# Four blocks of 240 rows instead of 256 in a mixture of experts behind an attention, and two more products at the start

## The chip, the cores and the metric

The kernel runs on one core of a Trainium2 chip. The metric is the device time of one execution in microseconds (us); lower is better. The time of a version is the median of several runs.

## The reference: what is computed

Two stages. A causal attention over 8 batches, 8 heads, 576 positions and 64 features per head, in which every key gets a bias from a running sum of `max(s, 0)`, gives 8 x 576 = 4608 tokens of 512 features. Each token then goes to exactly one of 8 experts, and the expert's two matrices (512 x 1024 and 1024 x 512) are applied with a ReLU between them:

```python
logits = np.einsum('bsd,de->bse', x, w_gate)
...
            fresh_e = int(np.argmax(logits[b, s]))
            if s == 0 or local_gate[b, s] < 0.5:
                e = fresh_e
            else:
                e = prev_e if prev_e >= 0 else fresh_e
...
            h = np.maximum(x[b, s] @ w1[e], 0.0)
            out[b, s] = p[e] * (h @ w2[e])
```

All numbers are float32. Which expert a token takes is known only on the chip, after its attention row is there. For the inputs of the reference (a fixed seed) the eight experts get 573, 516, 565, 575, 717, 459, 513 and 690 tokens; these counts are worked out from the reference itself.

## The kernel before, in words

**Attention.** `attention` (L736) goes through 32 pairs of heads. `scores` (L863) multiplies keys and queries into PSUM (L874), ScalarE takes the exponent (L875), GpSimd cuts the upper triangle (L860), and `values` (L894) multiplies the weights with V (L904). At the very start, before the first queries and keys have landed, `warm_up(6)` (L806 and L811) issues six products of a zero tile with itself on TensorE; each float32 product is two instructions in the trace, so they stand there as 12 (L809). The first pair's scores come next on TensorE's queue, then six transposes of the key weights (`key_weights`, L824; they wait for `key_exps`, L820, on ScalarE), whose copies on VectorE (L834) release the first weighted V tiles.

**Routing.** While the attention runs, a `Router` counts the tokens of each expert and stores each token's row into a table in DRAM, ordered by expert, with room for every expert.

**Experts.** `Experts` works through a fixed list of 23 units, the string `ORDER`. The sizes of a unit are fixed when the program is built; which expert and which rows of the table a unit takes is data, computed on VectorE and read into registers of the SyncE queue (`piece`, L482), where it becomes the address of a transfer.

- D is a double: 256 rows of one expert. S is 128 rows. M is two halves of 64 rows, T is a half and two quarters of 32 rows, and each piece has its own load of an expert.
- Before: 14 D, 5 S, 1 M, 3 T, in the order `DDDDDDDTDDTDDTDDSSMDSSS`. Units are numbered from 0.
- Every piece loads its expert's two matrices, 2 MB each (`load`, L501, issued at L520 on SyncE's queue), into one of four places; a load is issued when the place's last user is done (`ready` and `loads`, L667 and L679).
- `fetch` (L523) brings the rows from the table, and `turn_x` (L546) transposes them on VectorE (L552).
- `layer1` of D and S (L582) is, for each of 8 chunks of 128 hidden features, 4 products over the 512 features: the expert's first matrix is the stationary side, the rows are the moving side, 256 or 128 columns wide. ScalarE applies the ReLU (L584). As each float32 product is two instructions, a unit has 64 of them.
- `layer2` (L606): for each 128 rows, 8 products (16 instructions) in which the rows' hidden features are stationary (128 columns) and the second matrix moves, 512 columns wide. VectorE scales by the gate (L609) and GpSimd stores the rows to their tokens (L611).
- M and T do both layers with the rows stationary (L573 for the first), in column groups of 64 or 32, and `turn_h` (L586) transposes between them on VectorE.

**Who gets what.** `assign` (L379) takes, per expert, the number of pieces wanted and the number of pieces that there are, and gives the expert and the first row of each piece. It is called for doubles early (2, then 3 of them, while counts are still growing: `assign_early`), for the other 9 doubles (`assign_doubles`, L424), and for singles, halves and quarters (`assign_rest`, L434). What is over after a size goes to the next smaller one. The last two calls are put by hand into layer 1 of unit 1, behind its chunks 2 and 5 (`todo` in `run`, L619). If rows are left over at the end, `over` becomes positive, and a general version of the whole kernel runs behind a branch.

**Order of the work.** Every engine works through its own queue in program order. Behind the assignment on VectorE's queue stand `turn_x(2)`, which unit 2 needs, and the scaling of unit 1's results.

Of the kernel before, what the change touches and what calls it, by code (L numbers as in the profile page):

```python
# [10 lines left out]
I32 = mybir.dt.int32  # L11
Act = mybir.ActivationFunctionType
Alu = mybir.AluOpType
# [4 lines left out]
P = 128  # L18
B, H, S, DH = 8, 8, 576, 64
D = H * DH  # L20
E, F = 8, 1024
N = B * S
# [31 lines left out]
ROWS = E * CAP + 2 * P  # L54
EMPTY = 1 << 20
DOUBLE, SINGLE, HALF, QUARTER = 2 * P, P, P // 2, P // 4
EARLY = (2, 3)
PIECES = {"D": (DOUBLE,), "S": (SINGLE,), "M": (HALF, HALF), "T": (HALF, QUARTER, QUARTER)}
ORDER = "DDDDDDDTDDTDDTDDSSMDSSS"
UNITS_OF = {size: sum(PIECES[u].count(size) for u in ORDER) for size in (DOUBLE, SINGLE, HALF, QUARTER)}  # L60
PLACES = 4
SUM_MIN, SUM_MAX, ONE_MAX, END_MAX = 1e-19, 1e25, 1e12, 1e29

# [51 lines left out]
class Router:  # L115
# [294 lines left out]
    def assign_early(self, i):  # L410
# [3 lines left out]
        if i == 0:  # L414
            self.start, self.early = self.t("start", [P, E]), []
            of, self.used, _ = self.assign("a0", n, None, EARLY[0], DOUBLE)
        else:
# [4 lines left out]
        self.early.append(of)  # L422

    def assign_doubles(self):  # L424
        v = self.nc.vector
        self.counted()
        n = self.shifted("n1", 8)
        v.tensor_tensor(n, n, self.used, op=Alu.subtract)
        v.tensor_scalar(self.start, self.used, float(DOUBLE), None, Alu.mult)
        self.doubles, used, _ = self.assign("b", n, self.start, UNITS_OF[DOUBLE] - sum(EARLY), DOUBLE)  # L430
        v.tensor_tensor(self.used, self.used, used, op=Alu.add)
        v.tensor_scalar(self.start, self.used, float(DOUBLE), None, Alu.mult)

    def assign_rest(self):  # L434
        v = self.nc.vector
        n = self.shifted("n2", 7, QUARTER - 1)
        v.scalar_tensor_tensor(n, self.used, -2.0, n, Alu.mult, Alu.add)
        self.singles, used, _ = self.assign("c", n, self.start, UNITS_OF[SINGLE], SINGLE)
        v.scalar_tensor_tensor(self.used, self.used, 2.0, used, Alu.mult, Alu.add)
        v.tensor_scalar(self.start, self.used, float(SINGLE), None, Alu.mult)  # L440
        n = self.shifted("n3", 6, QUARTER - 1)
        v.scalar_tensor_tensor(n, self.used, -2.0, n, Alu.mult, Alu.add)
        self.parts, used, _ = self.assign("d", n, self.start, UNITS_OF[HALF], HALF)
        v.scalar_tensor_tensor(self.used, self.used, 2.0, used, Alu.mult, Alu.add)
        v.tensor_scalar(self.start, self.used, float(HALF), None, Alu.mult)
        n = self.shifted("n4", 5, QUARTER - 1)
        v.scalar_tensor_tensor(n, self.used, -2.0, n, Alu.mult, Alu.add)
        self.quarters, _, end = self.assign("q", n, self.start, UNITS_OF[QUARTER], QUARTER)
        self.over = self.t("over", [P, 1])
        v.tensor_scalar(self.over, end[:, E - 1 :], -float(UNITS_OF[QUARTER]), 0.0, Alu.add, Alu.max)  # L450


class Experts:
    def __init__(self, ctx, tc, w1, w2, out, table, router):
# [16 lines left out]
        loads = 0  # L471
        for kind in ORDER:
            at = []
            for size in PIECES[kind]:
                at.append((size, count[size]))
# [6 lines left out]
    def piece(self, u, i, row):  # L482
        size, n = self.units[u][1][i]
        r = self.router
        if size == DOUBLE:
            if n < sum(EARLY):
                j = int(n >= EARLY[0])
                of, n = r.early[j], n - j * EARLY[0]
            else:
                of, n = r.doubles, n - sum(EARLY)  # L490
        else:
            of = getattr(r, {SINGLE: "singles", HALF: "parts", QUARTER: "quarters"}[size])
        return self.nc.values_load(of[0:1, row, n : n + 1], engines=[ET.SP], min_val=0,
                                   max_val=E * CAP if row else E - 1,
                                   skip_runtime_bounds_check_because="clamped when it was counted")
# [27 lines left out]
    def fetch(self, u):  # L523
        if u >= len(self.units):
            return
        nc = self.nc
        kind = self.units[u][0]
        n = 2 if kind == "D" else 1
        xq = self.xq[u] = self.xqs.tile([P, 2 * DOUBLE // DH, XW], F32, name="xq")
        gi = self.gi[u] = self.sm.tile([P, 2, 2], F32, name="gi")  # L530

        def get(to, of):
            self.tc.add_to_no_dep_group("gets", nc.sync.dma_start(to, of).ins)

        first = 0
        for i, size in enumerate(PIECES[kind]):
            r = self.piece(u, i, 1)
            src = self.table[bass.ds(r, size)]
            t = slice(first // 32, (first + size) // 32)
            for a in range(4):  # L540
                get(xq[32 * a : 32 * a + 32, t, :], src[:, a, :].rearrange("(t i) f -> i t f", i=32))
            p = min(size, P)
            get(gi[first : first + p, :n, :], src[:, 0, XW - 2 :].rearrange("(n p) f -> p n f", p=p))
            first += size

    def turn_x(self, u):  # L546
        if u >= len(self.units):
            return
        n = 8 if self.units[u][0] == "D" else 4
        xq = self.xq.pop(u)  # L550
        xT = self.xT[u] = self.xts.tile([P, DK, DOUBLE], F32, name="xT")
        self.nc.vector.transpose(xT[:, :, : 32 * n].rearrange("p c (t i) -> p t c i", i=32),  # L552
                                 xq[:, :n, : P].rearrange("p t (c i) -> p t c i", i=32))
# [8 lines left out]
    def layer1(self, u, c):  # L562
        nc, mm = self.nc, self.nc.tensor.matmul
        kind, _, ls = self.units[u]
        xT = self.xT[u]
        if kind in "MT":
            if c == 0:
                self.hs[u] = self.fp.tile([P, F], F32, name="hs")
            if c < 2:
                ps = self.ps_m.tile([P, 512], F32, name="hp", tag="m")  # L570
                for k in range(DK):
                    for d, l in self.groups(u):
                        mm(ps[d, :], lhsT=xT[:, k, d], rhs=self.ws[l][0][:, k, c * 512 : c * 512 + 512],  # L573
                           start=(k == 0), stop=(k == DK - 1))
                nc.scalar.activation(self.hs[u][:, c * 512 : c * 512 + 512], ps, Act.Relu)  # L575
            return
        w = DOUBLE if kind == "D" else SINGLE
        if c == 0:
            self.hT[u] = self.fp.tile([P, FK, DOUBLE], F32, name="hT")
        ps = self.ps_h.tile([P, DOUBLE], F32, name="hp")  # L580
        for k in range(DK):
            mm(ps[:, :w], lhsT=self.ws[ls[0]][0][:, k, c * P : c * P + P], rhs=xT[:, k, :w],  # L582
               start=(k == 0), stop=(k == DK - 1))
        nc.scalar.activation(self.hT[u][:, c, :w], ps[:, :w], Act.Relu)  # L584
# [12 lines left out]
    def layer2(self, u, between=None):  # L597
        nc, mm = self.nc, self.nc.tensor.matmul
        kind, _, ls = self.units[u]
        hT = self.hT.pop(u)  # L600
        gi = self.gi.pop(u)
        for n in range(2 if kind == "D" else 1):
            ps = self.ps_y.tile([P, D], F32, name="yp")
            for k in range(FK):
                for d, l in self.groups(u):
                    mm(ps[d, :], lhsT=hT[:, k, n * P + d.start : n * P + d.stop], rhs=self.ws[l][1][:, k, :],  # L606
                       start=(k == 0), stop=(k == FK - 1))
            y = self.yp.tile([P, D], F32, name="y")
            nc.vector.tensor_scalar_mul(y, ps, gi[:, n, 1:2])  # L609
            nc.gpsimd.memset(self.router.gap, 0.0)  # L610
            put = nc.gpsimd.indirect_dma_start(  # L611
                out=self.out[:, :], out_offset=bass.IndirectOffsetOnAxis(ap=gi.bitcast(I32)[:, n, 0:1], axis=0),
                in_=y[:, :], element_offset=0, bounds_check=N - 1, oob_is_err=False, in_offset=None).ins
            self.tc.declare_no_dep(put, group="outs", reason="no two rows of the output are the same")
            self.tc.add_to_no_dep_group("outs", put)
            if between and not n:
                between()
# [118 lines left out]
def attention(ctx, tc, q, k, v, s, wx, ident, recs, wend, router, experts):  # L736
    nc = tc.nc
# [68 lines left out]
    def warm_up(n):  # L806
        warm = banks("warm")[:, 0]
        for i in range(n):
            mm(warm[:, :P], lhsT=zero, rhs=zero, start=True, stop=True)  # L809

    warm_up(6)  # L811

    nc.vector.tensor_scalar(s_sb, s_sb, 0.0, None, Alu.max)
    nc.vector.tensor_tensor_scan(cum, ones, s_sb, 0.0, op0=Alu.mult, op1=Alu.add)
# [122 lines left out]
    for g in range(NG - 1):  # L937
        m = HP * GB // 2 * (g + 1)
# [17 lines left out]
    m = NPAIR // 2  # L956
# [621 lines left out]
```

## Time and profile before

| what | value |
|---|---|
| median of 3 runs | 733.62 us (733.31 to 734.97) |
| the profiled execution | 753.2 us |
| its span, first to last instruction | 751.5 us |
| TensorE busy | 733.7 us, 98% of the span |
| VectorE, ScalarE, GpSimd busy | 253.2, 166.4, 207.0 us |
| layer 1 with rows moving (L582) | 1216 instructions, 234.1 us |
| layer 2 (L606) | 752 instructions, 259.3 us |
| mean traffic with HBM | 248 GB/s |
| granted TensorE clock, mean | 0.995 |

In the trace PE is TensorE's matmul, PEld its loading of the stationary side, DVE is VectorE, ACT ScalarE, POOL GpSimd and SP SyncE; a q behind the name means the engine's queue (it waits or issues a transfer). An instruction is named by the line of the kernel, what it writes and what it reads. The chain of waits is the work that ended last, followed back from the end: each piece is either the instruction before it on its engine, or what released it. What is not in the chain costs no time as long as it stays out of it. Layer 1 of the first unit begins at 223.6 us of the span; the experts fill the rest.

### The profile page before, as it was taken

Reading aid. Unit: us, or ns where it says so; the run is one execution under the profiler, and the core shown is the slowest. Engines: PE = TensorE matmul, PEld = TensorE weight load, DVE = VectorE, ACT = ScalarE, POOL = GpSimd, SP = SyncE. Lnnn points to the kernel's source line nnn. Section 1 sums busy time; section 2 is a strip of 40 time slices with the busy share of each in tenths; the row PEclk is TensorE's granted clock in tenths of the full one; section 3 lists DMA queues with packets and bytes.
Section 4 is the critical chain, followed back from the end, with each engine's and each line's share of the span. In section 5 each row is a group of like instructions: output and inputs, shape, how many; then the busy total and the mean of one; then the engine's idle time right before and its main releaser. Section 6 shows DMA issues by size and latency. Waiting matters only on the chain.

```text
span 751.5 us, 16161 instructions
## 1 busy us (share of the span) xinstructions
PE 733.7 (98%) x6517; PEld 502.5 (67%) x6517; DVE 253.2 (34%) x684; ACT 166.4 (22%) x355; POOL 207.0 (28%) x453
## 2 busy tenths in 40 slices
PE   9999999999989999999999999999999999999996
PEld 6888877878877567567657375537645676637674
DVE  4656668677756462101100511040132001050110
ACT  4545555355331011011001010101110111101110
POOL 3443367577575254340100001010101001000110
PEclk9999999999999999999999999999999999999998
DMA  8454464665639997698546979996999955899100
GB/s 280 165 176 159 142 199 150 199 214 170 187 88 363 356 397 221 235 425 211 229 145 204 375 235 423 303 388 255 427 309 381 426 193 228 283 386 359 36 15 32
DMA packets 57204, 187.28 MB, mean 249 GB/s; under 512 B 11869, under 2 KB 32093, under 8 KB 49568
## 3 DMA queue, kind: packets, MB, share of 16 engines
q1 hardware_dynamic: 50224, 165.91, 62.6%
q0 software_dynamic: 6800, 20.09, 7.0%
q8 instruction: 53, 0.87, 0.5%
q14 instruction: 31, 0.25, 0.1%
q10 hardware_dynamic: 96, 0.15, 0.1%
HBM read 165.50 MB, written 20.88 MB: 248 GB/s over the span
## 4 chain that ended last, share of the span: by engine, by line
PE 96%; issue 1%; DVE 1%; POOL 1%; DMA 1%; ACT 0%; SPq 0%; POOLq 0%; ACTq 0%
PE yp L606 34%; PE hp L582 31%; PE po L904 13%; PE ps L874 12%; PE hp L573 4%; PE lp L216 2%; DMA qb<-in_q_dram 1%; POOL table L348 0%; ACT e L875 0%; PE pos L300 0%; POOL e L860 0%; PE pos L301 0%; DVE xb L912 0%; SPq L769 0%; DVE y L609 0%
## 5 line engine op out<-in xcount | busy, mean ns | idle before, releaser
L606 PE MATMUL yp<-w2b,hT 128*128 128x512 f32 (+2 forms) x752 | 259.3, 593 | 0.0
L582 PE MATMUL hp<-xT,w1b 128*128 128x256 f32 (+1 forms) x1216 | 234.1, 353 | 0.0
L582 PEld LDWEIGHTS hp<-xT,w1b 128*128 128x128 f32 x1216 | 206.8, 191 | 32.9 <-issue 7.8
L606 PEld LDWEIGHTS yp<-w2b,hT 128*128 128x128 f32 (+2 forms) x752 | 107.9, 167 | 141.0 <-issue 139.6
L611 POOL DMA_INDIRECT out_dram<-y,gi x37 | 36.5, 986 | 416.8 <-DVE y L609 397.8
L584 ACT ACTIVATE hT<-hp 128x256 f32<-128x256 f32 (+1 forms) x152 | 54.0, 355 | 434.0 <-PE hp L582 420.8
L609 DVE TENSOR_SCALAR y<-yp,gi 128x512 f32<-128x512 f32 x37 | 27.6, 747 | 307.6 <-PE yp L606 307.6
L904 PE MATMUL po<-vg,e 128*64 128x66 f32 x3200 | 104.9, 223 | 7.0 <-issue 5.6
L875 ACT ACTIVATE e<-ps 128x768 f32<-128x768 f32 (+1 forms) x128 | 97.1, 837 | 47.1 <-PE ps L874 46.4
L904 PEld LDWEIGHTS po<-vg,e 128*64 128x64 f32 x3200 | 98.7, 138 | 13.0 <-issue 10.9
L874 PE MATMUL ps<-qb,kb 64*128 64x192 f32 (+4 forms) x768 | 98.1, 406 | 0.9 <-DMA qb<-in_q_dram 0.5
L874 PEld LDWEIGHTS ps<-qb,kb 64*128 64x128 f32 x768 | 66.2, 190 | 31.8 <-ACT e L875 15.2
L860 POOL TENSOR_SCALAR_AFFINE_SELECT e<-e 128x256 f32<-128x256 f32 (+1 forms) x160 | 67.3, 445 | 51.9 <-ACT e L875 50.8
L348 POOL DMA_INDIRECT table<-xb,idx x54 | 54.5, 1010 | 19.5 <-issue 17.2
L593 DVE STREAM_TRANSPOSE hT<-hs 32x256 f32<-32x256 f32 x64 | 27.9, 436 | 74.8 <-ACT hs L575 74.0
L854 DVE TENSOR_TENSOR vg<-va,wk 128x256 f32<-128x256 f32 x64 | 41.4, 711 | 0.0
L911 DVE RECIPROCAL recs<-po 128x12 f32<-128x12 f32 x64 | 13.5, 211 | 64.4 <-PE po L904 47.9
L552 DVE STREAM_TRANSPOSE xT<-xq 128x1024 f32<-128x1024 f32 (+1 forms) x23 | 23.7, 1028 | 16.5 <-DMA xq<-table 15.9
L573 PE MATMUL hp<-w1b,xT 128*32 128x512 f32 (+1 forms) x224 | 28.3, 594 | 0.0
L912 DVE TENSOR_TENSOR xb<-po,recs 128x384 f32<-128x384 f32 (+1 forms) x48 | 22.0, 458 | 1.9 <-POOL e L860 0.3
L573 PEld LDWEIGHTS hp<-w1b,xT 128*32 128x32 f32 (+1 forms) x224 | 8.1, 114 | 17.7 <-issue 17.6
L923 DVE STREAM_TRANSPOSE xt<-xb 128x576 f32<-128x576 f32 x24 | 17.1, 751 | 0.0
(229 smaller groups left out, 195.5 us busy)
## 6 DMA issues: line engine op xcount, KB each, us to landing
w2b<-in_w_dram SPq DMA_DIRECT2D x30, 2048.0 KB
w1b<-in_w_dram SPq DMA_DIRECT2D x29, 2048.0 KB
va<-in_v_dram SPq DMA_DIRECT2D x32, 320.0 KB
kb<-in_k_dram SPq DMA_DIRECT2D x31, 288.0 KB
qb<-in_q_dram SPq DMA_DIRECT2D x31, 288.0 KB
xq<-table SPq DMA_DIRECT2D x56, 130.0 KB
w1b<-in_w_dram SPq DMA_DIRECT2D x4, 512.0 KB
xq<-table SPq DMA_DIRECT2D x20, 65.0 KB
```

Of the source, the lines that this page charges most:

```text
L348: put = self.nc.gpsimd.indirect_dma_start(out=self.halves, in_=src, element_offset=0, in_offset=None, out_offset=bass.IndirectOffsetOnAxis ...
L573: mm(ps[d, :], lhsT=xT[:, k, d], rhs=self.ws[l][0][:, k, c * 512 : c * 512 + 512], start=(k == 0), stop=(k == DK - 1))
L582: mm(ps[:, :w], lhsT=self.ws[ls[0]][0][:, k, c * P : c * P + P], rhs=xT[:, k, :w], start=(k == 0), stop=(k == DK - 1))
L584: nc.scalar.activation(self.hT[u][:, c, :w], ps[:, :w], Act.Relu)
L593: self.nc.vector.transpose(hT[32 * a : 32 * a + 32, :, 32 * r : 32 * r + 32], hs[32 * r : 32 * r + 32].rearrange("p (c i) -> p c i", i=P)[ ...
L606: mm(ps[d, :], lhsT=hT[:, k, n * P + d.start : n * P + d.stop], rhs=self.ws[l][1][:, k, :], start=(k == 0), stop=(k == FK - 1))
L611: put = nc.gpsimd.indirect_dma_start(out=self.out[:, :], out_offset=bass.IndirectOffsetOnAxis(ap=gi.bitcast(I32)[:, n, 0:1], axis=0), in_= ...
L854: nc.vector.tensor_tensor(vg[:, to].rearrange("p c h e -> p (c h) e")[:, :, :DH], va[:, :c].rearrange("p c h e -> p (c h) e"), wk[:, n, to ...
L860: nc.gpsimd.affine_select(out=ap, in_=ap, compare_op=Alu.is_ge, fill=0.0, base=base, pattern=n, channel_multiplier=-1)
L874: mm(ps[:, h, at : at + z - a], lhsT=kb[d, key : key + P], rhs=qb[d, a:z], start=True, stop=True)
L875: nc.scalar.activation(e, ps, Act.Exp, scale=scale)
L904: mm(po[d, j - j0, :], lhsT=weights_of(n, c, j, h), rhs=vgs[n % NV][:, c if j < 2 * G1 else G1 + c, h, :], start=(c == 0), stop=(c == last))
```

## The change

Four of the 14 doubles become units of a new kind N, of 240 rows (`NARROW`): units 6, 9, 12 and 15. An N unit is a double in everything but this: the moving side of layer 1 is 240 columns wide, and the second part of layer 2 has 112 rows, so 112 stationary columns, and the scaling and the store take 112 rows. It still fetches, turns and indexes 256 rows.

Which experts get an N is decided on the chip in `assign_doubles`: `few` is 1 for an expert whose count minus one has bit 4 clear, which means that its last 32 rows hold 16 rows or fewer. Such an expert gets one N, if it still wants a double and there is one left. From then on, its count is raised by 16 (`cnt`), and the first row of its later pieces is lowered by 16 (`less`, `behind`). The remaining doubles, singles, halves and quarters are assigned as before.

The `warm_up` at the start issues 8 products instead of 6.

```diff
+NARROW = DOUBLE - QUARTER // 2
-ORDER = "DDDDDDDTDDTDDTDDSSMDSSS"
+ORDER = "DDDDDDNTDNTDNTDNSSMDSSS"
...
     def assign_doubles(self):
         v = self.nc.vector
         self.counted()
         n = self.shifted("n1", 8)
         v.tensor_tensor(n, n, self.used, op=Alu.subtract)
+        bit = self.s("bit", [P, E], I32)
+        v.tensor_scalar(bit, self.cnt, -1, None, Alu.add)
+        v.tensor_scalar(bit, bit, 4, None, Alu.logical_shift_right)
+        v.tensor_scalar(bit, bit, 1, None, Alu.bitwise_and)
+        few = self.s("few", [P, E])
+        v.tensor_copy(few, bit)
+        v.tensor_scalar(few, few, -1.0, 1.0, Alu.mult, Alu.add)
+        v.tensor_tensor(few, few, n, op=Alu.min)
         v.tensor_scalar(self.start, self.used, float(DOUBLE), None, Alu.mult)
+        self.narrows, narrow, _ = self.assign("w", few, self.start, UNITS_OF[NARROW], NARROW)
+        v.tensor_tensor(n, n, narrow, op=Alu.subtract)
+        v.scalar_tensor_tensor(self.start, narrow, float(NARROW), self.start, Alu.mult, Alu.add)
         self.doubles, used, _ = self.assign("b", n, self.start, UNITS_OF[DOUBLE] - sum(EARLY), DOUBLE)
         v.tensor_tensor(self.used, self.used, used, op=Alu.add)
-        v.tensor_scalar(self.start, self.used, float(DOUBLE), None, Alu.mult)
+        v.tensor_tensor(self.used, self.used, narrow, op=Alu.add)
+        self.less = self.t("less", [P, E])
+        v.tensor_scalar(self.less, narrow, float(DOUBLE - NARROW), None, Alu.mult)
+        whole = self.s("whole", [P, E])
+        v.tensor_tensor(whole, self.base, self.less, op=Alu.add)
+        v.tensor_tensor(self.cnt, whole, self.base0, op=Alu.subtract)
+        self.behind(DOUBLE)
+
+    def behind(self, size):
+        v = self.nc.vector
+        v.tensor_scalar(self.start, self.used, float(size), None, Alu.mult)
+        v.tensor_tensor(self.start, self.start, self.less, op=Alu.subtract)
...
 -        v.tensor_scalar(self.start, self.used, float(SINGLE), None, Alu.mult)
+        self.behind(SINGLE)
...
-        v.tensor_scalar(self.start, self.used, float(HALF), None, Alu.mult)
+        self.behind(HALF)
...
-            of = getattr(r, {SINGLE: "singles", HALF: "parts", QUARTER: "quarters"}[size])
+            of = getattr(r, {NARROW: "narrows", SINGLE: "singles", HALF: "parts", QUARTER: "quarters"}[size])
...
             r = self.piece(u, i, 1)
+            size = DOUBLE if size == NARROW else size
...
-        w = DOUBLE if kind == "D" else SINGLE
+        w = PIECES[kind][0]
...
-        for n in range(2 if kind == "D" else 1):
+        for n in range(2 if kind in "DN" else 1):
+            m = NARROW - P if kind == "N" and n else P
             ps = self.ps_y.tile([P, D], F32, name="yp")
             for k in range(FK):
                 for d, l in self.groups(u):
+                    d = slice(d.start, min(d.stop, m))
                     mm(ps[d, :], lhsT=hT[:, k, n * P + d.start : n * P + d.stop], rhs=self.ws[l][1][:, k, :],
                        start=(k == 0), stop=(k == FK - 1))
             y = self.yp.tile([P, D], F32, name="y")
-            nc.vector.tensor_scalar_mul(y, ps, gi[:, n, 1:2])
+            nc.vector.tensor_scalar_mul(y[:m], ps[:m], gi[:m, n, 1:2])
...
-    warm_up(6)
+    warm_up(8)
```

## The prediction

> **What bounds the kernel now.** I read first the shares of the chain that ended last, then the same chain in order of time (start, length, what):
>
> ```profile
> PE 96%; issue 1%; DVE 1%; POOL 1%; DMA 1%; ACT 0%; SPq 0%; POOLq 0%; ACTq 0%
> ```
>
> ```profile
> 6.35 4.28 PE ps L874 x20
> ...
> 381.95 13.73 PE yp L606 x32
> 395.68 13.81 PE hp L582 x64
> 409.49 7.00 PE hp L573 x64
> 416.50 20.93 PE yp L606 x96
> ...
> 702.67 7.14 PE hp L582 x64
> ```
>
> From 233.8 us to 744.8 us there is nothing but TensorE in this chain, one unit closing on the next: 395.68 + 13.81 = 409.49. A transfer, VectorE or ScalarE are never what ends last there. So in the experts' stage an instruction taken from TensorE comes off the end, until something else is late. Layer 1 of a double (L582) is 13.81 us for 64 instructions, 215.8 ns each for 256 columns; of a single (the last line) 7.14 / 64 = 111.6 ns for 128; layer 2 is 13.73 / 32 = 429.1 ns for 512. Between 256 and 512 a column costs 213.3 / 256 = 0.833 ns, between 128 and 256 it costs 0.814 ns.
>
> The groups of instructions, kept apart by shape, tell whether stationary loads matter (busy us, mean ns, idle before):
>
> ```profile
> L606 PE MATMUL yp<-w2b,hT 128*128 128x512 f32 x528 | 230.3, 593 | 0.0
> L606 PEld LDWEIGHTS yp<-w2b,hT 128*128 128x128 f32 x528 | 99.6, 190 | 120.6 <-issue 120.0
> ```
>
> A load takes 190 ns and the loader then idles about 240 ns, within the 429 ns of one product: it lies wholly beside the product.
>
> At the start TensorE is slow. Its timeline there:
>
> ```profile
> 2.78 1.27 PE L809 MATMUL warm<-xb 128*128 128x128 f32 x5
> 4.55 1.65 PE L874 MATMUL ps<-qb,kb 64*128 64x384 f32 x4 [0.49 <-DMA qb<-in_q_dram]
> 7.79 0.96 PE L874 MATMUL ps<-qb,kb 64*128 64x448 f32 x2
> 8.54 0.96 PE L874 MATMUL ps<-qb,kb 64*128 64x448 f32 x2
> 9.28 0.74 PE L874 MATMUL ps<-qb,kb 64*128 64x320 f32 x2
> ```
>
> Warming products of 128 columns begin 0.213 us apart (five in 1.27 us, of which the last takes 0.42), against 0.112 us in a single. Pairs of scores of 448 columns begin 0.75 us apart, 1.67 ns a column: half speed. It ends at about 10.2 us.
>
> **What the Trainium skill says.** "TensorE: Matmul & The Clock Gate", section "Back-to-back issue gap": a product's spacing at full clock is its columns at 2.4 GHz plus about 2.5 ns. With two array cycles a column, which is what this trace shows (0.833 ns), 240 columns are 200 + 2.5 = 202.5 ns; 256 would be 215.8, as measured. Section "LDWEIGHTS (loading the stationary operand)": loading time goes with the number of stationary columns, whatever the rows. The trace agrees in direction (190, 138 and 110 ns for 128, 64 and 32 columns), with a fixed part. Section "What's actually happening": the array runs at half clock until one window of about 3.4 us has been busy, and the windows run freely, not from the kernel's start. The trace agrees on the length: the clock falls once later, and from the stretches
>
> ```profile
> 232.00:234.00 2.00, 1.75 (x29) 1.49 (x30) 0.20 (x1) 0.00 (x0) 0.00 (x0) 0.52 0.93 374
> 234.00:236.00 2.00, 2.00 (x7) 1.62 (x7) 1.80 (x11) 0.00 (x0) 0.00 (x0) 0.62 1.06 448
> ```
>
> (the third number from the end is the granted clock) it was at half from 232.08 to 235.52, 3.4 us. Counting 65 such windows of 3.413 us back from 232.1 gives 10.25, just where the first speed-up stands. So windows ended here at 3.42, 6.84 and 10.25 us.
>
> **The change part by part.**
>
> *Do four experts qualify?* From the counts 573, 516, 565, 575, 717, 459, 513, 690, bit 4 of the count minus one is clear for 516, 717, 459 and 513: four experts. After the five early doubles each of them still wants one, so all four N are filled. Six doubles are then wanted and five are there, as ten and nine before. Singles 5, halves 6 wanted of 5, quarters 6 of 6 come out as before, nothing is left over. So the list of units does the same work in the same places, with 16 empty rows less in four of them.
>
> *Layer 1 of four N.* 16 columns less are 13.3 ns (0.833 x 16) an instruction, 64 instructions a unit, 4 units: 3.41 us; with 0.814 ns it is 3.33. That an odd width is charged by the column is seen in the attention: 66 columns, two column groups side by side, take 5.98 us for 200 instructions, 59.8 ns a pair against 55 + 2.5. The stationary loads here (190 ns) are as many as before and singles stream past them at 111.6 ns, so 202.5 ns is not below what they need. I take 3.4, all on the path.
>
> *Layer 2's second half, 112 stationary columns.* Still 16 instructions of 512 moving columns, 429 ns each: no gain. A load between 138 and 190 ns, about 177. No row shows 112 columns, so both ends: 0 if it hides like 128, or 64 loads x 0.177 = 11.3 us if none did. Nothing below zero, as the product's time is set by its moving side. I take 0: 64 and 32 columns hide as well. Scaling (747 ns) and store (986 ns) of 112 rows are off the path: 0.
>
> *Assignment on VectorE.* It adds 27 instructions in `assign_doubles` (6 for `few`, 14 for one more `assign`, 7 around) and 2 in `assign_rest`. The block now:
>
> ```profile
> 258.43 0.16 DVE L365 TENSOR_TENSOR cnt<-base,base 128x8 int32<-128x8 f32 x1
> ...
> 273.86 0.15 DVE L450 TENSOR_SCALAR over<-qend 128x1 f32<-128x1 f32 x1
> 274.31 1.25 DVE L552 STREAM_TRANSPOSE xT<-xq 128x1024 f32<-128x1024 f32 x1 [0.30 <-issue]
> 278.44 0.75 DVE L609 TENSOR_SCALAR y<-yp,gi 128x512 f32<-128x512 f32 x1 [2.89 <-PE yp L606]
> ```
>
> 80 instructions in 15.6 us, 0.195 each; 29 more are 5.7 us (4.9 to 7.0 with 0.17 to 0.24). Queued behind are `turn_x(2)`, then the scaling of unit 1. The turn ends at 281.3 instead of 275.6; unit 2's layer 1 wants it at 285.3, so 4 us of cover stay. The scaling at 278.4 slips to about 281.3; its PSUM buffer, one of two, is next wanted by unit 2's layer 2 at 299.3, and GpSimd's store of it and the table stores behind slip 3 us, for a fetch that SyncE issues at 341.8. SyncE first reads N's numbers for the load at 314.0 and the other doubles' at 299.3; both stand by about 268. Cost 0; if the cover were gone, the excess over 9.7 us would go straight to the path.
>
> *Do the weights keep up?* An N is ahead of each T, the unit with three loads, and takes 0.85 us from their lead. The tightest is unit 13:
>
> ```profile
> 518.32 2.56 SPq L520 DMA_DIRECT2D w2b<-in_w_dram  x3
> 521.46 0.33 SPq L520 DMA_DIRECT2D w1b<-in_w_dram  x1
> ```
>
> Four loads of 2.1 MB, 8.4 MB at the 409 to 422 GB/s that the stretches from 520 to 540 show, are 20 us: landed at about 541, used from 548.4. Seven us of cover against 0.85: cost 0. Fetches are unchanged.
>
> *Two more warming products.* Four instructions x 0.213 = 0.85 us: TensorE's stream of them ends at 4.71 instead of 3.85, and the first scores start at 4.71 instead of 4.55. This 0.16 is hidden, as the scores after the fourth wait for a transfer that lands at 6.30. What it may bring: in the window 3.42 to 6.84 TensorE streamed 0.43 + 1.41 + 0.49 = 2.33 of 3.41 us, 68%, and the clock stayed low. With the gap filled it is 3.07 us, 90%. No row shows whether 90% is enough. If so, full clock from 6.84, and the first pair's scores end up to 3.41 / 2 = 1.7 us earlier. ScalarE's timeline limits what comes through:
>
> ```profile
> 8.04 0.81 ACT L875 ACTIVATE e<-ps 128x768 f32<-128x768 f32 x1 [0.99 <-PE ps L874]
> 12.40 0.32 ACT L851 COPY vg<-wk 128x14 f32<-128x14 f32 x2 [0.91 <-DVE wk L834]
> ```
>
> Only the 0.99 us can shrink ahead of the key exponents; the transposes at 10.46 then come 1.2 earlier at most, and the rest follows. Ends: 0 (not raised) and 2.0 (an execution whose windows lie worse, where the second pair's scores were slow too). I take 1.0.
>
> *Sum.* 3.4 + 1.0 = 4.4 us: the profiled execution goes from 753.2 us to 748.8 (its span from 751.5 to 747.1). The median of the runs is 19.6 us lower than the profiled execution; columns over clock are the same in both, so I take off the same 4.4: 733.6 to 729.2.
>
> **The rivals.**
> - *Width only, the clock is not raised earlier.* For: 90% is not a full window, and windows lie differently in each execution. Against: the filled gap is nearly all that was missing. 733.6 - 3.4 = 730.2.
> - *Width does not pay* (240 columns cost what 256 do). For: no row shows 240. Against: 66 columns cost by the column. 732.6 with the warming, 733.6 without: no change.
> - *Slower: loads of 112 stationary columns are not drawn under the running product.* Place: 16 loads in each N's second half. Price 0.177 us x 64 = 11.3, so 733.6 - 4.4 + 11.3 = 740.5. It decides from 4.4 / 64 = 69 ns shown per load, and makes the kernel slower by over 0.2% from 92 ns. Against: every other width hides.
> - *It doesn't do what it says*: rows left over start the general kernel, and the time at least doubles (over 1467 us). The counts above leave this only if the chip chose otherwise.
>
> **How the numbers follow.** About 0.2%, 1.5 us, is what can be told from no change. Both parts work: 55%, 729.2. Width only: 32%, 730.2. Width does not pay: 7%. Exposed loads: 5%. Rows left over or the assignment's cover gone: 1%. Range: from 1.8 us below the first case (warming worth 2.0, and 0.8 for the scatter, as the runs shown span 1.66 us) to 1.2 above the second (scatter, and 232 us's fall of the clock, at most 1.7 us, which may come or go): 727.4 to 731.4; it leaves out 13% of cases and some tails. Faster 0.87, same 0.07, slower 0.06.
>
> **What would show it.** Layer 1 of units 6, 9, 12, 15 at 12.96 us instead of 13.81; their layer 2 still 13.73; no wait other than TensorE's in the chain from unit 1 on; the turn for unit 2 ending near 281 less the start's gain; pairs of 448 columns under 0.4 us apart at the start. Wrong would be: layer 2 of N above 13.8, a gap before unit 2, a weight wait before a T.

## The result, and the profile after

The changed kernel takes 731.51 us (median of 6 runs, 730.73 to 731.85); the kernel before, run beside it, takes 734.28 us (6 runs). The medians differ by 2.8 us. The ratio is 0.9957 with a 95% interval of 0.994 to 0.9973, which is 3.2 us faster, between 2.0 and 4.4. A second comparison on a chip with about the same times gave 0.9954 (0.9941 to 0.9967), and two on chips on which both kernels take longer gave 0.995 (0.9932 to 0.9968) and 0.9945 (0.9931 to 0.996). The profiled execution of the changed kernel took 731.85 us with a span of 730.1 us.

One thing has to be known before the two profiles are laid side by side. The profile of before (753.2 us) evidently came from another chip than its three runs (733.62 us). On such a chip the same kernel takes 750 us in its other executions as well (experiment `b6_again`). So the 21 us between the two spans are mostly the chip, not the change, and stages are compared by their lengths, not by their place in the span. There is no trace of the kernel before from a chip on which it takes 734 us.

The shares of the chain that ended last are as before:

```profile
PE 96%; DMA 1%; ACT 1%; DVE 1%; issue 1%; POOL 0%; POOLq 0%; DVEq 0%; ACTq 0%
```

The same chain in order of time (start, length, what), at unit 6, which is an N, then the next two pieces, and later unit 15, an N with its own layer 2 behind it:

```profile
377.54 12.96 PE hp L608 x64
390.50 7.00 PE hp L599 x64
397.50 20.93 PE yp L634 x96
...
583.47 12.96 PE hp L608 x64
596.43 13.73 PE yp L634 x32
```

Layer 1 of an N is 12.96 us where a double's was 13.81; its layer 2 is 13.73 as before, and the pieces still close on one another (583.47 + 12.96 = 596.43). The groups by shape (busy us, mean ns, idle before) show the two new shapes:

```profile
L608 PE MATMUL hp<-xT,w1b 128*128 128x240 f32 x256 | 52.5, 366 | 0.0
L634 PE MATMUL yp<-w2b,hT 128*112 128x512 f32 x64 | 28.1, 592 | 0.0
L634 PEld LDWEIGHTS yp<-w2b,hT 128*112 128x112 f32 x64 | 11.3, 177 | 16.1 <-issue 16.1
```

The loads of 112 stationary columns take 177 ns, as estimated, and the loader idles 16.1 us before 64 of them, 0.25 us each: they hide under the product, whose mean is 592 ns as the others' is 593.

VectorE's timeline over the longer assignment, and TensorE's at the place that waits for it:

```profile
240.29 0.16 DVE L366 TENSOR_TENSOR cnt<-base,base 128x8 int32<-128x8 f32 x1
...
261.06 0.15 DVE L475 TENSOR_SCALAR over<-qend 128x1 f32<-128x1 f32 x1
261.15 1.25 DVE L578 STREAM_TRANSPOSE xT<-xq 128x1024 f32<-128x1024 f32 x1
```

```profile
266.96 3.40 PE L608 MATMUL hp<-xT,w1b 128*128 128x256 f32 x15
```

From the first instruction of the assignment to the turn it is 20.9 us instead of 15.9, and the turn ends at 262.4, 4.6 us before unit 2 begins.

TensorE's timeline at the start:

```profile
6.58 0.54 PE L902 MATMUL ps<-qb,kb 64*128 64x448 f32 x2
6.96 0.54 PE L902 MATMUL ps<-qb,kb 64*128 64x448 f32 x2
```

The pairs of 448 columns begin 0.38 us apart instead of 0.75: the clock has risen. The trace's record of the granted clock has it at 5.12 us, against 10.23 in the trace of before.

### The profile page after: what moved, and what is told of

It reads as the page before. It is cut to its first block, busy times and chain, and to the rows that moved or that the text cites. A ratio compares the mean times of both kernels' runs of the same rounds, so it can differ in the third digit from the quotient of the medians.

```text
span 730.1 us, 16198 instructions
## 1 busy us (share of the span) xinstructions
PE 719.0 (98%) x6521; PEld 496.6 (68%) x6521; DVE 258.4 (35%) x713; ACT 165.4 (23%) x355; POOL 206.1 (28%) x453
## 4 chain that ended last, share of the span: by engine, by line
PE 96%; DMA 1%; ACT 1%; DVE 1%; issue 1%; POOL 0%; POOLq 0%; DVEq 0%; ACTq 0%
PE yp L634 35%; PE hp L608 31%; PE po L932 12%; PE ps L902 11%; PE hp L599 4%; PE lp L217 1%; DMA table<-xb,idx 1%; ACT e L903 1%; PE warm L837 1%; DVE xb L940 0%; PE pos L301 0%; POOL e L888 0%; POOL table L349 0%; PE pos L302 0%; DVE y L637 0%
## 5 line engine op out<-in xcount | busy, mean ns | idle before, releaser
L634 PE MATMUL yp<-w2b,hT 128*128 128x512 f32 (+3 forms) x752 | 259.3, 593 | 0.0
L608 PE MATMUL hp<-xT,w1b 128*128 128x256 f32 (+2 forms) x1216 | 229.8, 349 | 0.0
L634 PEld LDWEIGHTS yp<-w2b,hT 128*128 128x128 f32 (+3 forms) x752 | 107.1, 166 | 141.8 <-issue 140.2
L610 ACT ACTIVATE hT<-hp 128x256 f32<-128x256 f32 (+2 forms) x152 | 53.4, 352 | 425.4 <-PE hp L608 425.4
L637 DVE TENSOR_SCALAR y<-yp,gi 128x512 f32<-128x512 f32 (+1 forms) x37 | 27.6, 745 | 304.8 <-PE yp L634 298.5
L932 PE MATMUL po<-vg,e 128*64 128x66 f32 x3200 | 98.5, 223 | 2.2 <-issue 1.2
L932 PEld LDWEIGHTS po<-vg,e 128*64 128x64 f32 x3200 | 95.5, 138 | 5.1 <-issue 3.7
L902 PE MATMUL ps<-qb,kb 64*128 64x192 f32 (+4 forms) x768 | 94.1, 397 | 0.5 <-ACT e L903 0.3
## 6 DMA issues: line engine op xcount, KB each, us to landing
w1b<-in_w_dram SPq DMA_DIRECT2D x29, 2048.0 KB, 10.1
```

The source lines that it names most:

```text
L902: mm(ps[:, h, at : at + z - a], lhsT=kb[d, key : key + P], rhs=qb[d, a:z], start=True, stop=True)
L932: mm(po[d, j - j0, :], lhsT=weights_of(n, c, j, h), rhs=vgs[n % NV][:, c if j < 2 * G1 else G1 + c, h, :], start=(c == 0), stop=(c == last))
```

## The experiments

Theory A: the width is worth all of its 3.4 us, and the two more warming products little. Theory B: the warming is worth 1.0 us or more, and a part of the width is eaten by a wait. The runs stand in three groups, each on one chip, on which the kernel before was timed as well; ratios are against it. In the first two groups it takes about 750 us, in the third (from `w8_move` on) 734.5.

| run | what it is | median us | before | ratio (95%) |
|---|---|---|---|---|
| b6_again | before, once more | 751.53 | 750.05 | 1.0009 (0.9992 to 1.0027) |
| w6_width | N units, 6 products | 747.31 | 750.05 | 0.9959 (0.9945 to 0.9973) |
| b8_warm | doubles, 8 products | 750.67 | 750.05 | 0.9998 (0.9981 to 1.0015) |
| w8_again | the changed kernel | 746.98 | 750.05 | 0.9950 (0.9932 to 0.9968) |
| w8_n224 | layer 1 of N on 224 columns; leaves out its last 16 rows | 743.46 | 750.63 | 0.9918 (0.99 to 0.9936) |
| w6_width2 | as w6_width | 745.11 | 750.63 | 0.9936 (0.9918 to 0.9954) |
| w8_again2 | the changed kernel | 746.07 | 750.63 | 0.9945 (0.9931 to 0.996) |
| w8_late | loads 1 and 2 of the experts put behind chunk 5 | 745.95 | 750.63 | 0.9946 (0.9931 to 0.9962) |
| w8_move | last projection two chunks later | 730.46 | 734.47 | 0.9943 (0.993 to 0.9955) |
| w8_again3 | the changed kernel | 731.11 | 734.47 | 0.9954 (0.9941 to 0.9967) |
| w0_width | N units, no warming product | 731.54 | 734.47 | 0.9960 (0.9945 to 0.9975) |
| w8_spin | 60 more additions on VectorE | 739.66 | 734.47 | 1.0069 (1.0052 to 1.0087) |

### b6_again: which execution was the exception

No edit.

> The kernel before, once more, for its trace and as a measure of the scatter: ratio 1.000 within 0.2%. Theory A (the first traced execution of it, 753 us, was an exception): its span here is about 732 us, layer 1 of the first unit begins near 211 to 213 us instead of 223.6, and no stretch at half clock stands between attention and experts, or one that costs up to 4 us. Theory B (tracing costs 20 us in that version): 751 us again.

Neither theory as it was worded. Its traced execution has a span of 751.5 us, but the others of this kernel take 750 to 751 us here too (medians). Tracing costs nothing that can be seen; the chip does. Between attention and experts its chain has this, as the trace of before had:

```profile
229.55 1.17 issue
230.72 0.25 PE lp L216
...
233.65 9.71 PE hp L582 x40
243.36 6.87 PE yp L606 x16
```

"issue" is TensorE waiting for nothing that the profile shows. In the changed kernel's trace from the other chip the same stretch is without it:

```profile
215.04 1.46 PE lp L217 x64
216.50 8.83 PE hp L608 x40
225.33 6.87 PE yp L634 x16
```

From the beginning of the first unit to that of the second it is 34.1 us in the trace of before and 29.9 us in this one. 0.88 of the difference is 9.71 against 8.83 for the same 40 instructions: in the trace of before the clock stood at half from 232.10 to 235.51 us, over the first 1.75 us of them. This stretch is a part of what the two chips differ by; the larger part, 223.6 against 209.7 us, lies before the first unit.

### w6_width and b8_warm: one part each

```diff
-    warm_up(8)
+    warm_up(6)
```

> The four units of 240 rows alone, with six warming products. Theory A (the width is worth all of its 3.4 us, the two more warming products bring nearly nothing in most executions): 3.4 us less than before, ratio 0.9954. Theory B (the warming brings its 1.0 us and the width is eaten by a wait): 1.5 to 2 us less, ratio about 0.9975. In the trace both want layer 1 of an N at 12.96 us.

0.9959 is 3.1 us, the 3.4 of Theory A within its interval (2.0 to 4.1 us); layer 1 of the N units stands at 12.96 us.

```diff
-    warm_up(6)
+    warm_up(8)
```

> Eight warming products alone, all doubles of 256 rows. Theory A: within 0.5 us of before, ratio 0.9995 to 1.0005, although the clock rises in the first pair's scores in the trace. Theory B: 1.0 us less or more, ratio 0.9986 or below. Scores of 448 columns begin 0.37 us apart if the clock has risen, 0.75 if not.

0.9998: no difference, between 1.4 us faster and 1.1 slower. Its trace has the clock up at 5.66 us, and scores of 448 columns 0.37 us apart. So the clock does what the warming is for, and the time does not show it. That is as Theory A had it, but the interval still holds the 1.0 us of Theory B.

### w8_again, w6_width2, w8_again2: is there anything in the warming?

No edits beyond those above.

> The changed kernel, once more, on the same chip as the three others: ratio 0.9957 as measured (2.8 to 3.4 us less). Theory A: equal to the width alone within 0.5 us. Theory B: 1 us below the width alone.

> The width alone once more, beside the changed kernel on this chip. Theory A (warming is worth the 1.0 us that the trace shows at the start): 1.0 us slower than the changed kernel. Theory B (the start's gain is given back before the experts begin): equal to it within 0.3 us.

> The changed kernel once more: ratio 0.995 to 0.9957. Theory A: 1.0 us below the width alone. Theory B: equal within 0.3 us.

By the medians, the changed kernel is 0.3 us below the width alone in the first group, as Theory A of `w8_again` had it, and 1.0 above it in the second, which no theory had. All 28 executions of the width alone have a mean of 747.0 us, the 33 of the changed kernel 746.6: 0.4 us, with a standard error of 0.45. `b8_warm` has 0.0 with 0.46 in the same way (14 executions against 48). Together that is 0.2 with 0.3: 1.0 us is unlikely, though neither comparison alone rules it out.

In the traces from these chips the lead is there. The second slot of scores (behind the first two pairs' scores) begins at 20.2 to 20.7 us with six products (four traces) and at 19.1 to 19.8 with eight (five traces), and the first unit begins at 222.5 us in the mean of the four against 221.6 in the mean of the five, still 0.9 us apart. Single traces of one version differ by up to 2 us at that point, so the traces do not tell where the lead goes, or whether it goes.

### w8_n224: is every column paid?

```diff
-        w = PIECES[kind][0]
+        w = PIECES[kind][0] - (16 if kind == "N" else 0)
...
+            if kind == "N":
+                nc.gpsimd.memset(self.hT[u][:, :, w:NARROW], 0.0)
```

> The changed kernel with layer 1 of the four N units cut to 224 columns (it leaves out layer 1 of the last 16 rows of each N; those hidden features are set to zero). Theory A (every column is paid at 0.833 ns, nothing else is near): layer 1 of an N at 64 x 189.2 ns = 12.11 us, another 3.4 us less than the changed kernel, ratio about 0.991. Theory B (something else than the columns is close, such as loads or the ReLU): 12.5 us or more, less than 1.7 us gained.

The chain of its trace:

```profile
390.42 12.11 PE hp L610 x64
```

12.11 us, exactly as expected: 13.81, 12.96 and 12.11 for 256, 240 and 224 columns, 0.85 us for each 16. Its median is 2.6 us below the changed kernel's on the same chip, against 3.4 in the trace; the means differ by 3.3 with a standard error of 0.8, which covers it. Down to 224 columns nothing else limits layer 1.

### w8_late: are the weights' transfers to blame for the waits at the hand-over from attention to experts?

```diff
-            (0, 0): [lambda: self.load(0, 1, behind=self.hT[0][0:1, 0, 0:1]), lambda: self.load(1), lambda: router.assign_early(1), lambda: self.load(2)],
+            (0, 0): [lambda: self.load(0, 1, behind=self.hT[0][0:1, 0, 0:1])],
+            (0, 5): [lambda: self.load(1), lambda: router.assign_early(1), lambda: self.load(2)],
```

> The changed kernel, but the weights of experts' loads 1 and 2 (8 MB) are issued after chunk 5 of unit 0's layer 1 instead of after chunk 0. Theory A (at the hand-over from attention to experts TensorE is starved by that burst of transfers, goes idle, and its clock falls to half for 3.4 us in some executions): the waits at L217 between 227 and 232 us and the half-clock stretch vanish, 1 to 3 us less than the changed kernel and less scatter. Theory B (the waits there have another cause): same as the changed kernel within 0.5 us.

Equal to the changed kernel (745.95 against 746.07), and the waits stand where they stood, with the half clock behind them. Its chain:

```profile
228.28 0.37 issue
228.64 0.34 PE lp L217 x3
228.99 0.39 issue
...
232.08 10.52 PE hp L608 x40
```

But the edit did not take the transfers away from this place. SyncE's timeline, and the stretch of 2 us in which the waits begin (the last two numbers are the busy share of the DMA engines and GB/s):

```profile
225.65 0.35 SPq L545 DMA_DIRECT2D w1b<-in_w_dram  x1
226.37 0.54 SPq L545 DMA_DIRECT2D w2b<-in_w_dram  x1
242.78 0.33 SPq L545 DMA_DIRECT2D w1b<-in_w_dram  x1
```

```profile
228.00:230.00 2.00, 0.86 (x20) 0.23 (x8) 0.00 (x0) 0.00 (x0) 1.70 (x3) 1.00 1.02 431
```

Load 1 went out at 225.65 and 226.37 us, as in the trace of `w8_again2` (225.02 and 226.46): SyncE has a queue of its own, and nothing in it waits for chunk 5. Only load 2 came later, at 242.78 instead of 227.93, because it waits for `assign_early`, which was moved with it. So the DMA engines were busy all through the waits, and Theory A was not put to the test. Two other traces speak against it. In the trace of before, TensorE has waits of the same kind between 189.3 and 191.0 us, where the DMA engines are busy for 0.26 of the time:

```profile
189.30:191.00 1.70, 0.86 (x14) 0.55 (x13) 0.00 (x0) 0.00 (x0) 0.97 (x1) 1.00 0.26 95
```

And `w8_move`, below, goes through the same instructions without a wait beside a full stream of transfers, though on the other kind of chip.

### w8_move, w8_again3, w0_width: a chip without those waits

```diff
-            (0, 2): [lambda: router.product(last, self.xts_of, self.banks, (1,)),
+            (0, 4): [lambda: router.product(last, self.xts_of, self.banks, (1,)),
```

> The changed kernel, but the last group's projection and what hangs on it (product, logits, codes and the two turns) stands behind chunk 4 of unit 0's layer 1 instead of chunk 2. Theory A (TensorE's waits of 2 to 3 us at L217 come from its queue of short instructions not being filled fast enough right behind the attention, and lead to the fall of the clock): fewer or no waits at L217, no stretch at half clock, 1 to 3 us less than the changed kernel. Theory B (they come with the product wherever it stands): same as the changed kernel within 0.5 us.

> The changed kernel once more, as the measure for the others on this chip: ratio 0.9945 to 0.9957.

These runs were made on a chip of the shorter time, whose traces have no wait at L217 and no half clock there, before the move or after it. So neither theory was put to the test. The stretch with L217 in the trace of `w8_move` has TensorE busy for all of its 1.40 us, at a DMA share of 1.05:

```profile
217.50:218.90 1.40, 1.40 (x65) 1.25 (x65) 0.00 (x0) 0.38 (x1) 1.24 (x3) 1.00 1.05 431
```

Its 730.46 us is the lowest of all and 0.65 us below the changed kernel, with intervals that overlap. From the first unit on, both traces last 520.2 us, so the move itself gave nothing that the trace shows.

```diff
-    warm_up(8)
```

> The four N units without any warming product. Theory A (six products never raised the clock before the first pair's scores were through, so none is as good as six): clock up at about 10.2 us in the trace as with six, time equal to the width alone, 0 to 1.0 us above the changed kernel. Theory B (warming in itself is worth something beyond that): the clock rises later, past 11 us, and it is 2 us or more above the changed kernel.

731.54 against 731.11 us: 0.4 us, as on the other chips, and no more certain (the means differ by 0.5 with a standard error of 0.6). Theory A's time came, Theory B's 2 us did not; the clock did neither. Without any warming the clock rose at 8.18 us, earlier than in the four traces with six products (10.1 to 10.4), as TensorE's timeline shows:

```profile
4.46 1.65 PE L901 MATMUL ps<-qb,kb 64*128 64x384 f32 x4 [4.46 <-DMA qb<-in_q_dram]
...
7.83 0.72 PE L901 MATMUL ps<-qb,kb 64*128 64x448 f32 x2
8.38 0.54 PE L901 MATMUL ps<-qb,kb 64*128 64x448 f32 x2
```

The second pair of 448 columns begins 0.55 us behind the first, between the 0.75 of half clock and the 0.38 of full clock: the rise at 8.18 us falls into the first.

### w8_spin: what the cover before unit 2 is worth

```diff
-            (1, 5): [router.assign_rest],
+            (1, 5): [router.assign_rest, self.spin],
...
+        for _ in range(60):
+            self.nc.vector.tensor_tensor(pad, pad, self.router.less, op=Alu.add)
```

> The changed kernel with 60 more small additions on VectorE behind the assignment, about 12 us. The cover left before unit 2 is 4.6 us in the changed kernel's trace: layer 1 of unit 2 begins 7 to 8 us later, with a wait of that length for the turn of its rows, and nothing of it is won back. If instead VectorE's block were not on that path: no change.

TensorE's timeline, and after it the stretches of 5 us (granted clock third from the end):

```profile
272.61 2.93 PE L608 MATMUL hp<-xT,w1b 128*128 128x256 f32 x6 [7.19 <-DVE xT L578]
```

```profile
265.00:270.00 5.00, 0.42 (x1) 0.00 (x0) 4.15 (x26) 0.00 (x0) 0.00 (x0) 0.87 0.81 275
270.00:275.00 5.00, 2.39 (x6) 1.95 (x7) 4.71 (x13) 0.00 (x0) 1.40 (x3) 0.50 0.43 180
```

The 60 additions took 12.0 us. From unit 1 to unit 2 it is 34.9 us instead of 27.5: 7.4 us longer, which is 12.0 less the 4.6 of cover. The idle TensorE also lost its clock, from 268.7 to 275.5 us, which cost some 1.5 us more (from unit 2 to unit 6 it is 111.9 us against 110.4). Together that is 8.9; the median of its two runs is 8.55 us above the changed kernel's.

## Why the prediction was right, and where its sizes were off

**The forecast** was 729.2 us, 4.4 below the median then known; the result is 731.51, 0.1 above the upper end of the stated range. The base accounts for 0.66 of the gap: three more runs moved the median of before from 733.62 to 734.28. The gain is 2.8 us by the medians and 3.2 by the ratio (2.0 to 4.4), and by the ratio 3.2 to 4.1 over the four comparisons. So the direction and the larger term came as worked out, and the smaller term was set too high. In size the result stands nearer to the rival "width only" (3.4 us), but not for that rival's reason: the clock was raised earlier, and the time did not follow.

**From the profiled execution to the median.** The forecast of 748.8 us for the profiled execution cannot be compared with the 731.85 measured, as the two profiles come from different kinds of chip. That the same 4.4 us might be taken off the median was an assumption; for the width it held, as the N units gain on both kinds.

**Four experts qualify; layer 1 of four N.** Right to the digit: 12.96 us each, 3.4 us in all (`w8_n224` adds that the slope holds below 240). They lie in the chain that ended last, and the width alone is 3.1 us (2.0 to 4.1) and 4.8 (3.5 to 6.2) faster where the kernel takes 750 us, and 2.9 (1.8 to 4.0, against a before that has six warming products where this one has none) where it takes 734.

**112 stationary columns.** Right: 177 ns as interpolated, all hidden, layer 2 unchanged at 13.73 us. The rival on the slower side, exposed loads, falls by the same line.

**Assignment on VectorE.** Mechanism and size right: 5.0 us longer where 5.7 was worked out, 4.6 us of cover left where 4 was. `w8_spin` shows that this was a real path: the excess over the cover came through whole, and the clock lost in the wait on top of it.

**Weights.** No wait for a load stands before unit 7, 10 or 13 in the chain. The last load that unit 13 needs is issued at 501.67 us and its first product begins at 527.78, 26.1 us later instead of 27.0: the 0.85 us less lead that the prediction allowed for.

**Two more warming products.** This is the term that was mis-sized: 1.0 us in the sum, 0.4 with a standard error of 0.45 beside N units and 0.0 with 0.46 beside doubles in the runs. The step "if 90% is enough, full clock from 6.84" was right in kind: with eight products the clock was up at 4.0 to 7.1 us in all nine traces, and the lead of about 1 us is there at the second slot. What the times do not bear out is "the rest follows", that such a lead is found whole at the end. The traces still have 0.9 us of it, in the mean, at the first unit; behind that the hand-over differs from trace to trace by more than the lead. Where it goes is not settled.

**The 90% that no row showed.** The runs bring the bound nearer, if windows of 3.413 us (the length of the half-clock stretch in the trace of before) are counted back from each rise, and streaming is counted as the prediction did: the last product of a stretch ends one spacing after its start. TensorE's timelines of `w8_again3` and, below it, of `w6_width`:

```profile
1.13 3.40 PE L837 MATMUL warm<-xb 128*128 128x128 f32 x16 [1.13 <-DVE xb L816]
```

```profile
1.13 2.93 PE L837 MATMUL warm<-xb 128*128 128x128 f32 x12 [1.13 <-DVE xb L816]
4.62 4.43 PE L902 MATMUL ps<-qb,kb 64*128 64x384 f32 x16 [0.56 <-DMA qb<-in_q_dram]
```

In the first the clock rose at 4.00 us, so its window began at 0.58, and TensorE streamed from 1.13 on: 84% was enough. In the second it rose at 10.29; in the window from 3.46 to 6.88 TensorE streamed to 3.85 and again from 4.62, which is 78%, and this was not enough. The bound hangs on the way of counting: by the recorded ends, which lie some 0.2 us later, both windows have 84%.

**The step that was not foreseen** is the size of what may come and go at the hand-over. The prediction gave it 1.7 us. The traces have 29.8 to 35.1 us from the first unit to the second, and on the 750 us chips the executions of before whose mean granted clock was 0.996 or less (27 of 75) were 2.6 us longer than the others. That is why one comparison was not enough for a change of 0.4%.

## What to carry to other kernels

On an engine that closes on itself from end to end, work taken away comes off the end at its own price, column by column, as long as each neighbour's cover is counted first: here 5 us of new VectorE work was free only because 9.7 us of cover stood before it, and the same work 60 instructions longer cost all that was over. A gain in the first microseconds of a long kernel is not yet a gain at its end: here about 1 us at the start was 0.2 us, with a standard error of 0.3, in the times. And before two profiles are laid side by side, the same kernel should be seen twice: two chips differed by 16 us here, over five times the change. Last, an experiment that is to move a transfer should be read first at the queue that issues it: `w8_late` moved its lines in the program and only one of its two loads in time.

## What had not been expected of the hardware

- The same program takes 734 us on one chip and 750 on another. TensorE's waits among short instructions, which nothing in the profile releases ("issue"), are a part of it: between 15 and 240 us the nine traces from chips of the longer time have 14 to 16 waits of over 0.3 us, 5.6 to 6.9 us in sum and at nearly the same instructions, and the five from the others have one to three, 0.5 to 1.8 us in sum. The cause of the waits stays open, and so does what makes up the rest of the 16 us; `w8_late` left one of the suspected transfers where it was, and whether moving the projection helps was not tried on such a chip.
- The Trainium skill ("TensorE: Matmul & The Clock Gate", section "What's actually happening") lets the clock rise after a busy window of 3.4 us on a grid that runs freely. Traces agree with the grid: in the one of before, the later fall comes 221.87 us, 65 windows of 3.413, after the rise. The runs add that a window need not be full (84% did, 78% did not, as counted above), and that with six products the rise stood at 10.1 to 10.4 us four times of four, with none at 8.2 and with eight between 4.0 and 7.1, more closely together for six than a free grid would lead one to expect.
- In a wait of TensorE of 7.2 us, from 265.4 to 272.6 us, the clock fell to half, and stayed there for 6.8 us, two such windows: the trace of `w8_spin` records it from 268.66 to 275.49 us.
